# A Strassen block's accumulating transfer behind the next block's operand sums, and its transpose as a work list of its own

## The chip, the cores and the metric

The kernel runs on one core of a Trainium2 chip. The metric is the device time of one execution in microseconds (us), taken as the median of several runs; lower is better. A profile is one more execution, recorded by the hardware profiler.

## The reference

Two layers follow each other. The first is a causal depthwise convolution over the sequence: eight heads of 24 channels, seven taps per head, the taps normalized by a softmax. The second is a feed-forward layer with exact Gelu, 192 to 2048 to 192 channels.

```python
# x: (8, 4096, 192), weight: (8, 7), w_in: (192, 2048), w_out: (2048, 192), float32
w = exp(weight - max(weight)); w = w / (sum(w) + 1e-9)      # per head
out = einsum('hk,bskhg->bshg', w, windows of 7 of x padded in front)
h = out.reshape(32768, 192) @ w_in
return (0.5 * h * (1 + erf(h / sqrt(2)))) @ w_out
```

## The kernel before

The 32768 tokens are taken as two halves that are worked on side by side, and each half is cut into 35 blocks: six of 256 tokens (numbers 0 to 5) and 29 of 512 (6 to 34). For each block n the stages are these, and different engines work on different blocks at one time.

- SP loads x into `xin` (`load`, L571) and stores results from `osb` (`store`, L591).
- VectorE transposes x (`trans`, L748) and does the convolution as seven multiply-add steps of two parts each (`conv`, L776, written c in the order). ScalarE does the first tap of most blocks (L865). GpSimd copies the six columns of overlap between blocks (`halo`, L670).
- TensorE multiplies by w_in (`mm1`, L992) in 16 slices per block. ScalarE's Gelu (L897) takes each slice from PSUM `hp` to `gT`.
- In the slices of block n, TensorE also multiplies block n - 1 by w_out: for most blocks in the plain way (`mm2_t`, L1070), and for the thirteen blocks of the list `ST` (8, 10, ..., 32) with one level of Strassen's scheme (`mm2_s`, L1130). So the even blocks hold `mm2_t` of an odd block, and the odd blocks hold `mm2_s` of an even one.

A Strassen block m needs sums of its Gelu outputs as matmul operands, kept in the four tiles `sst`: S1, S3, Dn and S4, where Dn is made from S1 and S4 from Dn. S1 and S3 have four parts each, Dn and S4 two. Five of these sums are done by DMA from GpSimd's queue: a plain copy of the first term (`st_dma`, L495), then an accumulating transfer of the second (L498), ten transfers in all. VectorE does the rest (`st_add`, L488): S1 parts 2 and 3, S3 part 3, and all of Dn and S4. TensorE meets them in the odd block: S1 at its start, S3 next, then S4 (from slice 6).

After the products, block m's results are put together. ScalarE copies four pieces (`st_copy`, L526: `gsm`, `p5s`, `uu` and the negated half of `uu`). VectorE adds in four steps (`st_post`, called POST 0 to 3 here: L535, L539, L542, L546). GpSimd issues three moves (`st_move`): p5s (L505), gsm (L507), and the accumulating `tq += uu` (L510, 256 KB). Then three 512-column tiles are transposed into `osb` (`st_evac`, L561): j = 2 from PSUM, j = 1 from `tq` after that accumulating transfer, and j = 0 from `gsm`. The plain blocks have three such transposes (`evac_t`, L376), which also free PSUM banks for the Strassen products.

Two orders are fixed by hand. VectorE's is the string `ORDER`: each letter takes the next entry of a list (t transpose, c convolution step, p POST, e evacuation, and 1, 3, d, 4 for the sums of S1, S3, Dn, S4). GpSimd's is a list sorted by (block, place): the halo copy of a block, then that block's gsm and tq moves of the Strassen block before, then the ten operand transfers. Every wait on a semaphore holds all that is queued behind it on the same engine. S_EV counts evacuations; `EVC[n]` is its value before block n's.

Of the kernel before, what the change touches and what calls it, by code (L numbers as in the profile page):

```python
# [11 lines left out]
def bass_lightweight_conv__then__act_gelu_exact_kernel(  # L12
# [23 lines left out]
    NA = 5  # L36
# [3 lines left out]
    NP = D // 64  # L40
# [26 lines left out]
    NG = [w // 128 for w in WS]  # L67
# [3 lines left out]
    M0, M1 = 6, NB - 1  # L71
    ST = list(range(M0 + 2, M1, 2))
# [3 lines left out]
    for n in range(NB):  # L76
        new = M0 <= n < M1
        PHC.append(PHC[n] + (0 if n in ST else 2 if new else 3 * NG[n] if n == 0 else NG[n]))
        MMC.append(MMC[n] + (1 if new else 2 * NG[n] if n == M1 else NG[n]))
        EVC.append(EVC[n] + (0 if n < NA else NP if new else NG[n]))  # L80

# [32 lines left out]
    def sem(name):  # L116
        return es.enter_context(nc.semaphore(name))
# [4 lines left out]
    with es:  # L122
# [65 lines left out]
        S_DP = sem("S_DP")  # L188
        BY_DMA = [("S3", 0), ("S1", 0), ("S3", 1), ("S1", 1), ("S3", 2)]
        DMAS = [(3, "S3", 0, 0), (4, "S1", 0, 0), (5, "S3", 0, 1), (7, "S3", 1, 0), (8, "S1", 1, 0),  # L190
                (8.1, "S1", 0, 1), (10, "S1", 1, 1), (11, "S3", 2, 0), (11.1, "S3", 1, 1), (13, "S3", 2, 1)]
        S_CP = {k: sem("S_CP_%s_%d" % k) for k in BY_DMA}
        S_AD = {k: sem("S_AD_%s_%d" % k) for k in BY_DMA}
        S_PS = sem("S_PS")
        S_GU = sem("S_GU")
        S_TQ = sem("S_TQ")

        block = es.enter_context(nc.Block())

# [106 lines left out]
        def wait_ev(e, m, g):  # L306

            if m < NA:
                e.wait_ge(S_EVA, G0[m] + g + 1)
            else:  # L310
                e.wait_ge(S_EV, EVC[m] + g + 1)

        def wait_banks(t, m, g):

            k = G0[m] + g
            if m < M0:
                if k >= 2:
                    t.wait_ge(S_EVA, k - 1)
            elif g % 2:
                t.wait_ge(S_GELU, SL0[NB] - 1 + g // 2)  # L320
            elif M1 - 1 in ST:
                i = ST.index(M1 - 1)
                t.wait_ge(*((S_AC, 4 * i + 3) if g == 0 else (S_EV, EVC[M1] - 2)))
                t.wait_ge(S_DP, 4 * i + 3 + g // 2)
            else:
                t.wait_ge(S_EV, EVC[M1] - 2 + g)
# [92 lines left out]
        def osb_t(m, j):  # L419
            return ap(osb[m % 2], j, [[8 * C, 128], [C // 2, TB // 32], [NP, 32]])  # L420
# [91 lines left out]
        def st_copy(a, m, k):  # L512

            def xb(r, w=TB):
                return bank(BK[m]["X"], r, w)

            if k == 0 and m != ST[0]:
                a.wait_ge(S_EV, EVC[ST[ST.index(m) - 1] + 1])
            if k < 3:
                st_done(a, m, ("P1", "P5", "P6")[k])  # L520
            else:
                a.wait_ge(S_AC, 4 * ST.index(m) + 3)
            dst, src = (
                (gsm[LO, :], xb(LO)), (p5s[UP, :], xb(UP)), (uu[LO, :], xb(LO)), (uu[UP, :], uu[LO, :]),
            )[k]
            a.activation(out=dst, in_=src, func=AF.Copy, scale=-1.0 if k == 3 else 1.0).then_inc(S_AC)  # L526
# [22 lines left out]
        def st_evac(v, m, j):  # L549
            i = ST.index(m)  # L550
            if j == 2:
                st_done(v, m, "DE")
                v.wait_ge(S_OUT[m % 2], OUTS[m - 2])
                src = bank(BK[m]["D"])
            elif j == 1:
                v.wait_ge(S_TQ, 16 * (i + 1))
                src = tq[:, :]
            else:
                v.wait_ge(S_DP, 4 * i + 4)
                src = gsm[:, :]  # L560
            v.transpose(osb_t(m, j), src).then_inc(S_EV)  # L561

        def load(e, n, qs=(0, 2, 1, 3), sm=None):
            mb = WS[n] // 32
# [10 lines left out]
        def store(e, m):  # L575
            if m < M0:
                for g in range(NG[m]):
                    wait_ev(e, m, g)
                    e.dma_start(
                        ap(  # L580
                            outt,
                            (OFF[m] + 128 * g) * C,
                            [[C, 128], [HALF * C, 2], [1, C]],
                        ),
                        ap(osb[m % 2], g * C, [[8 * C, 128], [4 * C, 2], [1, C]]),
                    ).then_inc(S_OUT[m % 2], 16)
                return
            wait_ev(e, m, NP - 1)
            for q in range(4):

                e.dma_start(  # L591
                    ap(
                        outt,
                        ((q // 2) * HALF + OFF[m]) * C + (q % 2) * (C // 2),
                        [[C, 32], [32 * C, WS[m] // 32], [1, C // 2]],
                    ),
                    ap(
                        osb[m % 2],
                        32 * q * 8 * C,
                        [[8 * C, 32], [C // 2, WS[m] // 32], [1, C // 2]],  # L600
                    ),
                ).then_inc(S_OUT[m % 2], 16)
# [1 line left out]
        TAPS = ((5, 8, 11), (10, 12, 15))  # L604
        ORDER = (
            "tccccccccccccctccctccccccccccccwtccccccccccccwwwwwctcccccccccccctcccccccccccccccccccccccccettceccccc"
            "cccccccccetccccecccccccetcecc1ccde13de44ccccccpctpcpeccccccccpccececet1cccde13de44cccccpcccptpcecccc"
            "ccccpccececet1cccde13de44cccccpcccptpceccccccccpccececet1cccde13de44cccccpcccptpceccccccccpccececet1"
            "cccde13de44cccccpcccptpceccccccccpccececet1cccde13de44cccccpcccptpceccccccccpccececet1cccde13de44ccc"
            "ccpcccptpceccccccccpccececet1cccde13de44cccccpcccptpceccccccccpccececet1cccde13de44cccccpcccptpceccc"  # L610
            "cccccpccececet1cccde13de44cccccpcccptpceccccccccpccececet1cccde13de44cccccpcccptpceccccccccpccececet"
            "1cccde13de44cccccpcccptpceccccccccpccecececc1ccde13de44ccccccpcppepeeeeeeeee"
        )
        AT_COPY = {0: (1, 6), 1: (1, 8), 2: (1, 13), 3: (2, 1)}

# [1 line left out]
        def _(g):  # L617
# [73 lines left out]
            for m in ST:  # L691
                for at, name, q, h in DMAS:
                    work.append(((m, at), st_dma, g, m, name, q, h))
                work += [((m + 1, 8.5), st_move, g, m, 0), ((m + 2, 2), st_move, g, m, 1), ((m + 2, 3), st_move, g, m, 2)]
            for _, op, *rest in sorted(work, key=lambda q: q[0]):
                op(*rest)

# [1 line left out]
        def _(v):  # L699
# [98 lines left out]
            for j in range(3, len(pieces(1))):  # L798
# [6 lines left out]
                "p": [(st_post, v, m, k) for m in ST for k in range(4)],  # L805
                "e": [(evac, v, M0 - 1, g) for g in range(NG[M0 - 1])],
            }
            for c, name in zip("13d4", NS):
                lanes[c] = [(st_add, v, m, name, q) for m in ST for q in BY_V[name]]
            for m in range(M0, M1):  # L810
                lanes["e"] += [(st_evac, v, m, 2 - j) if m in ST else (evac_t, v, m, j) for j in range(NP)]
            lanes["e"] += [(evac_half, v, g, 0) for g in range(NG[M1])]
            for c in ORDER:
                op, *rest = lanes[c].pop(0)
# [96 lines left out]
        def _(t):  # L911
# [135 lines left out]
            def mm2_t(m, ps, i):  # L1047

                w = WS[m]
                if i == 0:  # L1050
                    if m - 1 in ST:
                        s = ST.index(m - 1)
                        if ps == 0:
                            t.wait_ge(S_AC, 4 * s + 3)
                            t.wait_ge(S_DP, 4 * s + 3)
                        elif ps == 1:
                            t.wait_ge(S_EV, EVC[m] - 2)
                    elif ps < 2:
                        t.wait_ge(S_EV, EVC[m] - (1 if m == M0 else 2) + ps)
                    if ps > 0:  # L1060
                        t.wait_ge(S_PH, PHC[m] + ps)
                if ps == 0 and i % 4 == 0:

                    t.wait_ge(S_GELU, SL0[m] + i + 4)
                for hf in range(2):
                    j = UPLO[ps][hf]
                    r = slice(64 * hf, 64 * hf + 64)
                    for h in range(2):
                        c0 = (2 * i + h) * w
                        ins = t.matmul(  # L1070
                            bank(BK[m][j], slice(64 * h, 64 * h + 64), w),
                            ap(
                                wout,
                                64 * hf * NF * C + CH[h][i] * C + j,
                                [[NF * C, 64], [NP, 64]],
                            ),
                            gT[m % 2][r, c0 : c0 + w],
                            start=(i == 0 and (ps == 0 or (ps, hf) == (1, 1))),
                            stop=(i == NF - 1 and (ps == 2 or (ps, hf) == (1, 0))),
                            tile_position=(64 * hf, 64 * h),  # L1080
                        )
                if i == NF - 1:
                    ins.then_inc(S_MM2 if ps == 2 else S_PH)
# [94 lines left out]
            m = NB - 1  # L1178
# [67 lines left out]
```

## Time and profile before

| what | value |
|---|---|
| median of 3 runs | 671.94 us (670.77 to 674.0) |
| profiled execution | 676.62 us |
| its span, first to last instruction | 674.9 us |
| granted TensorE clock | 1.00 |
| busy share: PE, DVE, ACT, POOL | 99%, 91%, 88%, 28% |
| even blocks of the Strassen stretch (first Gelu to first Gelu) | 20.53 us |
| odd blocks of it | 19.88 to 22.12 us |

Span and times inside it come from the profiled execution; 1.7 us of its time lie outside the span. A busy share is an average over all stages. An entry such as "DVE sst L488 <- DMA sst<-gT" reads: VectorE sat idle before its instruction of line 488, which writes `sst`, until a DMA that writes `sst` from `gT` had landed.

### The profile page before, as it was taken

Reading aid. Unit: us, or ns where it says so; the run is one execution under the profiler, and the core shown is the slowest. Engines: PE = TensorE matmul, PEld = TensorE weight load, DVE = VectorE, ACT = ScalarE, POOL = GpSimd, SP = SyncE. Lnnn points to the kernel's source line nnn. Section 1 sums busy time; section 2 is a strip of 40 time slices with the busy share of each in tenths; the row PEclk is TensorE's granted clock in tenths of the full one; section 3 lists DMA queues with packets and bytes.
Section 4 is the critical chain, followed back from the end, with each engine's and each line's share of the span. In section 5 each row is a group of like instructions: output and inputs, shape, how many; then the busy total and the mean of one; then the engine's idle time right before and its main releaser. Section 6 shows DMA issues by size and latency. Waiting matters only on the chain.

```text
span 674.9 us, 27462 instructions
## 1 busy us (share of the span) xinstructions
PE 666.3 (99%) x12504; PEld 498.6 (74%) x12504; DVE 612.9 (91%) x704; ACT 594.4 (88%) x681; POOL 191.4 (28%) x230
## 2 busy tenths in 40 slices
PE   9899999999999999999999999999999999999998
PEld 8899655565676776767777777876777777777787
DVE  5999998889998999999999999999999999999621
ACT  8799988898897988989899898988989899898883
POOL 7000702314142151421414325051240514324000
DMA  9436352686945769467695776958578785746433
GB/s 155 107 87 140 73 107 58 137 168 155 188 121 116 171 152 191 126 126 162 152 196 131 153 160 127 194 125 180 127 147 173 164 166 147 143 111 153 101 73 94
DMA packets 159075, 93.72 MB, mean 139 GB/s; under 512 B 129088, under 2 KB 152448, under 8 KB 158960
## 3 DMA queue, kind: packets, MB, share of 16 engines
q1 hardware_dynamic: 129136, 49.37, 33.7%
q0 software_dynamic: 28704, 42.02, 28.9%
q8 instruction: 98, 1.61, 1.0%
q10 hardware_dynamic: 1120, 0.59, 0.3%
q14 instruction: 17, 0.14, 0.1%
HBM read 28.31 MB, written 25.17 MB: 79 GB/s over the span
## 4 chain that ended last, share of the span: by engine, by line
PE 77%; DMA 10%; ACT 5%; DVE 3%; POOL 2%; issue 2%; DVEq 0%; POOLq 0%
PE hp L992 38%; PE ob L1070 17%; PE ob L1130 16%; DMA sst<-gT 9%; PE ob L1032 4%; ACT gT L897 4%; DVE sst L488 1%; DMA xin<-in_x_dram 1%; PE ob L1186 1%; PE hp L1186 1%; DMA win<-in_moe_w_in_dram 1%; POOL sst L498 1%; ACT acc L865 1%; DVE acc L776 1%; ACT uu L526 1%
## 5 line engine op out<-in xcount | busy, mean ns | idle before, releaser
L897 ACT ACTIVATE gT<-hp 128x1024 bf16<-128x1024 f32 x510 | 514.0, 1021 | 67.0 <-PE hp L992 61.3
L992 PE MATMUL hp<-xc,win 64*64 64x512 bf16 (+2 forms) x6036 | 447.2, 366 | 1.1 <-DVE xc L776 1.0
L992 PEld LDWEIGHTS hp<-xc,win 64*64 64x64 bf16 (+1 forms) x6036 | 238.6, 106 | 86.0 <-ACT gT L897 7.7
L776 DVE SCALAR_TENSOR_TENSOR acc<-xT,wcol,acc 128x1024 f32<-128x1024 f32 (+1 forms) x330 | 298.0, 963 | 4.0 <-ACT acc L865 3.1
L1070 PE MATMUL ob<-gT,wout 64*64 64x512 bf16 x2880 | 205.0, 376 | 0.0
L1130 PE MATMUL ob<-gT,wout 64*64 64x512 bf16 x1248 | 174.1, 377 | 0.0
L1070 PEld LDWEIGHTS ob<-gT,wout 64*64 64x64 bf16 x2880 | 118.2, 118 | 39.9
L1130 PE MATMUL ob<-sst,wst 64*64 64x512 bf16 x624 | 131.2, 377 | 2.3 <-DVE sst L488 1.3
L498 POOL DMA_DIRECT2D sst<-gT x65 | 85.6, 1317 | 97.6 <-DMA sst<-gT 94.3
L1130 PEld LDWEIGHTS ob<-gT,wout 64*64 64x64 bf16 x1248 | 86.1, 118 | 18.6
L748 DVE STREAM_TRANSPOSE xT<-xin 128x1536 f32<-128x1536 f32 (+2 forms) x39 | 74.5, 1921 | 4.0 <-DMA xin<-in_x_dram 3.9
L488 DVE TENSOR_TENSOR sst<-gT,sst 128x2048 bf16<-128x2048 bf16 x52 | 61.9, 1213 | 8.0 <-DMA sst<-gT 7.3
L495 POOL DMA_DIRECT2D sst<-gT x65 | 54.8, 858 | 30.1 <-ACT gT L897 28.5
L1130 PEld LDWEIGHTS ob<-sst,wst 64*64 64x64 bf16 x624 | 53.2, 107 | 13.2 <-DVE sst L488 3.7
L776 DVE SCALAR_TENSOR_TENSOR xc<-xT,wcol,acc 128x1024 bf16<-128x1024 f32 (+1 forms) x66 | 61.7, 958 | 0.1
L670 POOL COPY xT<-xT 128x18 f32<-128x18 f32 x30 | 29.1, 971 | 113.6 <-DVE xc L776 106.3
L865 ACT ACTIVATE acc<-xT,wcol 128x512 f32<-128x512 f32 (+1 forms) x87 | 61.0, 702 | 0.0
L1130 PE MATMUL ob<-gT,wst 64*64 64x512 bf16 x208 | 57.5, 377 | 1.1 <-DVE tq L535 1.0
L376 DVE STREAM_TRANSPOSE osb<-ob 128x512 f32<-128x512 f32 x45 | 40.4, 901 | 12.2 <-PE ob L1070 12.1
L1130 PE MATMUL ob<-sst,wout 64*64 64x256 bf16 x416 | 45.6, 269 | 0.0
L1032 PE MATMUL ob<-wout,gT 64*128 64x192 bf16 x768 | 41.3, 243 | 0.8 <-issue 0.8
L505 POOL DMA_DIRECT2D p5s<-p5s x13 | 7.4, 571 | 113.8 <-ACT p5s L526 113.8
(74 smaller groups left out, 320.1 us busy)
## 6 DMA issues: line engine op xcount, KB each, us to landing
sst<-gT POOLq DMA_DIRECT2D x130, 256.0 KB, 4.4
out_dram<-osb SPq DMA_DIRECT2D x124, 192.0 KB, 4.0
xin<-in_x_dram SPq DMA_DIRECT2D x116, 192.0 KB, 4.2
tq<-uu POOLq DMA_DIRECT2D x13, 256.0 KB, 4.0
xin<-in_x_dram SPq DMA_DIRECT2D x18, 96.0 KB, 2.5
gsm<-uu POOLq DMA_DIRECT2D x13, 128.0 KB, 2.2
p5s<-p5s POOLq DMA_DIRECT2D x13, 64.0 KB, 4.8
wout<-in_moe_w_out_dram POOLq DMA_DIRECT2D x4, 192.0 KB, 5.0
```

The source lines that it names most:

```text
L376: v.transpose(osb_t(m, j), bank(BK[m][j])).then_inc(S_EV)
L488: v.tensor_tensor(out, one, two, ALU.add).then_inc(S_SA[NS.index(name)])
L495: e.dma_start(out, one).then_inc(S_CP[name, q], 16)
L498: e.dma_start(out, two, accum_op=ALU.add).then_inc(S_AD[name, q], 16)
L748: v.transpose(out, src).then_inc(S_TR)
L776: ins = v.scalar_tensor_tensor(dst, src, wk, a, op0=ALU.mult, op1=ALU.add)
L865: a.activation(out=acc[n % 2][:, p * TB : p * TB + w], in_=ap(xT[n % 2], p * XW + HX, [[NP * XW, 128], [1, w]]), func=AF.Copy, scale=wcol[ ...
L897: a.activation(out=ap(gT[n % 2], i * c * 2 * w, dst), in_=ap(ob, 2 * TB, [[4 * TB, 128], *src[1:]]) if u < SL0[1] and u % 3 == 2 else ap(h ...
L992: ins = t.matmul(hbuf(u, slice(fo, fo + fw), o, w), ap(win, f1, [[NP * F, 64], [2, fw]]), xc[n % 2][r, p * TB : p * TB + w], start=(p == 0 ...
L1032: ins = t.matmul(bb[sub], gT[m % 2][r, c0 : c0 + 128], wout[r, CH[sub][i] * C : (CH[sub][i] + 1) * C], start=(ph == 0 and k == 0), stop=(p ...
L1070: ins = t.matmul(bank(BK[m][j], slice(64 * h, 64 * h + 64), w), ap(wout, 64 * hf * NF * C + CH[h][i] * C + j, [[NF * C, 64], [NP, 64]],), ...
L1130: ins = t.matmul(bank(BK[m][bk], slice(64 * cg, 64 * cg + 64), w), wt_, a[r, c0 : c0 + w], start=(e == mine[0]), stop=(e in (mine[-1], GRO ...
```

## The change

The accumulating transfer `tq += uu` of Strassen block m was issued by GpSimd ahead of the ten operand transfers of block m + 2. It now stands behind the last of them (place 14.1 in place of 3; the last operand transfer's place is renumbered from 13 to 14). Only the last Strassen block, which has no successor, keeps its place.

The transpose that reads `tq` leaves the list of evacuations, in which it stood between j = 2 and j = 0. It becomes a list of its own, q, with a semaphore of its own, S_ET. In `ORDER` it comes between the two S4 sums of block m + 2 (for block 30 behind both). In the same string one convolution step moves from behind the S4 sums to ahead of the first Dn sum, the next x transpose comes before the first bank's transpose in place of behind it, and the second bank's transpose comes behind S1 part 3.

S_EV now counts two evacuations for a Strassen block, and the waits on it are renumbered. The store of a Strassen block waits for S_ET as well, and so does ScalarE's first copy of the next Strassen block.

```diff
-        EVC.append(EVC[n] + (0 if n < NA else NP if new else NG[n]))
+        EVC.append(EVC[n] + (0 if n < NA else 2 if n in ST else NP if new else NG[n]))
...
-                (8.1, "S1", 0, 1), (10, "S1", 1, 1), (11, "S3", 2, 0), (11.1, "S3", 1, 1), (13, "S3", 2, 1)]
+                (8.1, "S1", 0, 1), (10, "S1", 1, 1), (11, "S3", 2, 0), (11.1, "S3", 1, 1), (14, "S3", 2, 1)]
...
             if k == 0 and m != ST[0]:
                 a.wait_ge(S_EV, EVC[ST[ST.index(m) - 1] + 1])
+                a.wait_ge(S_ET, ST.index(m))
...
-            v.transpose(osb_t(m, j), src).then_inc(S_EV)
+            v.transpose(osb_t(m, j), src).then_inc(S_ET if j == 1 else S_EV)
...
-            wait_ev(e, m, NP - 1)
+            wait_ev(e, m, (1 if m in ST else NP - 1))
+            if m in ST:
+                e.wait_ge(S_ET, ST.index(m) + 1)
...
     one period of ORDER:
-    pccececet1cccde13de44cccccpcccptpcecccccccc
+    pcccectec1cccd1e3de4q4ccccpcccptpcecccccccc
...
-                work += [((m + 1, 8.5), st_move, g, m, 0), ((m + 2, 2), st_move, g, m, 1), ((m + 2, 3), st_move, g, m, 2)]
+                work += [((m + 1, 8.5), st_move, g, m, 0), ((m + 2, 2), st_move, g, m, 1)]
+                work.append(((m + 2, 3 if m == ST[-1] else 14.1), st_move, g, m, 2))
...
+            lanes["q"] = [(st_evac, v, m, 1) for m in ST]
...
-                lanes["e"] += [(st_evac, v, m, 2 - j) if m in ST else (evac_t, v, m, j) for j in range(NP)]
+                lanes["e"] += [(st_evac, v, m, j) for j in (2, 0)] if m in ST else [(evac_t, v, m, j) for j in range(NP)]
...
-                            t.wait_ge(S_EV, EVC[m] - 2)
+                            t.wait_ge(S_EV, EVC[m] - 1)
```

More of the change, by code (lines that the diff above doesn't have):

```diff
@@ L196, in bass_lightweight_conv__then__act_gelu_exact_kernel @@
         S_TQ = sem("S_TQ")
+        S_ET = sem("S_ET")
         block = es.enter_context(nc.Block())
@@ L322, in wait_banks @@
                 i = ST.index(M1 - 1)
-                t.wait_ge(*((S_AC, 4 * i + 3) if g == 0 else (S_EV, EVC[M1] - 2)))
+                t.wait_ge(*((S_AC, 4 * i + 3) if g == 0 else (S_EV, EVC[M1] - 1)))
                 t.wait_ge(S_DP, 4 * i + 3 + g // 2)
@@ L606, in bass_lightweight_conv__then__act_gelu_exact_kernel @@
             "tccccccccccccctccctccccccccccccwtccccccccccccwwwwwctcccccccccccctcccccccccccccccccccccccccettceccccc"
[L607 to L612, printed above, removed]
+            "cccccccccetccccecccccccetcecc1ccde13de44ccccccpctpcpeccccccccpcccectec1cccd1e3de4q4ccccpcccptpcecccc"
+            "ccccpcccectec1cccd1e3de4q4ccccpcccptpceccccccccpcccectec1cccd1e3de4q4ccccpcccptpceccccccccpcccectec1"
+            "cccd1e3de4q4ccccpcccptpceccccccccpcccectec1cccd1e3de4q4ccccpcccptpceccccccccpcccectec1cccd1e3de4q4cc"
+            "ccpcccptpceccccccccpcccectec1cccd1e3de4q4ccccpcccptpceccccccccpcccectec1cccd1e3de4q4ccccpcccptpceccc"
+            "cccccpcccectec1cccd1e3de4q4ccccpcccptpceccccccccpcccectec1cccd1e3de4q4ccccpcccptpceccccccccpcccectec"
+            "1cccd1e3de4q4ccccpcccptpceccccccccpcccececc1ccde13de44qccccpcccppepeqeeeeeee"
         )
```

## The prediction

> **What bounds the kernel now.** First the page: busy times, then the chain that ended last.
>
> ```profile
> PE 666.3 (99%) x12504; PEld 498.6 (74%) x12504; DVE 612.9 (91%) x704; ACT 594.4 (88%) x681; POOL 191.4 (28%) x230
> PE 77%; DMA 10%; ACT 5%; DVE 3%; POOL 2%; issue 2%; DVEq 0%; POOLq 0%
> ```
>
> TensorE carries the chain, so only time in which TensorE waits can be won. It can hardly be read from 99%, so I cut the span at the first Gelu of each 512-token block. Even blocks take 20.53 us, all of them. Odd blocks, in which TensorE runs the Strassen products of the block before, take 20.06 us undisturbed; six take longer. One of each (a stretch, its length, busy time by engine):
>
> ```profile
> core 0: us, PE busy (x) PEld busy (x) DVE busy (x) ACT busy (x) POOL busy (x), PEclk, DMA share, GB/s
> 210.05:232.17 22.12, 20.86 (x393) 14.44 (x388) 20.13 (x22) 18.81 (x23) 2.47 (x4) 1.00 0.80 168
> 500.12:520.18 20.06, 20.06 (x393) 15.24 (x388) 19.87 (x22) 18.81 (x23) 2.42 (x4) 1.00 0.83 176
> ```
>
> Block 27 (from 500.12) is TensorE without a hole; block 13 (from 210.05) loses 2.06 us. The other losers are blocks 11, 15, 17, 23 and 25 with 1.19, 1.15, 1.58, 0.46 and 0.68: 7.1 us in all, over a floor of 674.9 - 7.1 = 667.8 us of span. That is the most that can be won. Below, times with a sign count from the first Gelu of the odd block.
>
> Who ends TensorE's waits between 150 and 310 us:
>
> ```profile
> DVE sst L488 <- DMA sst<-gT: 6.7, 4, 2.5
> PEld ob L1130 <- DVE sst L488: 3.2, 4, 0.8
> PEld ob L1130 <- DVE tq L535: 2.7, 4, 0.7
> PEld ob L1130 <- DMA sst<-gT: 2.6, 4, 1.2
> ```
>
> So VectorE's sums wait for the DMA sums, and TensorE for both. VectorE in block 13, then GpSimd:
>
> ```profile
> 206.31 2.63 DVE L776 SCALAR_TENSOR_TENSOR acc<-xT,wcol,acc 128x512 f32<-128x512 f32 x3
> 211.42 1.23 DVE L488 TENSOR_TENSOR sst<-gT,sst 128x2048 bf16<-128x2048 bf16 x1 [2.48 <-DMA sst<-gT]
> 212.56 0.89 DVE L376 STREAM_TRANSPOSE osb<-ob 128x512 f32<-128x512 f32 x1
> 213.33 1.24 DVE L488 TENSOR_TENSOR sst<-gT 128x1024 bf16<-128x1024 bf16 x2
> 216.40 2.29 DVE L488 TENSOR_TENSOR sst<-gT,sst 128x2048 bf16<-128x2048 bf16 x2
> 218.63 4.98 DVE L776 SCALAR_TENSOR_TENSOR acc<-xT,wcol,acc 128x1024 f32<-128x1024 f32 x5
> 223.64 0.69 DVE L535 TENSOR_TENSOR tq<-ob,p5s 64x512 f32<-64x512 f32 x1
> ```
> ```profile
> 192.03 0.95 POOL L510 DMA_DIRECT2D tq<-uu  x1
> 193.45 0.74 POOL L495 DMA_DIRECT2D sst<-gT  x1 [0.47 <-ACT gT L897]
> 205.49 1.20 POOL L498 DMA_DIRECT2D sst<-gT  x1 [3.35 <-DMA sst<-gT]
> 212.32 1.20 POOL L498 DMA_DIRECT2D sst<-gT  x1 [3.67 <-DMA sst<-gT]
> ```
>
> VectorE idles 2.48 us before the first Dn sum (211.42), until the accumulate of S1 part 1 (issued at 205.49) has landed. The sums after it and POST 0 (L535, 223.64) are late by as much. Over the odd blocks one rule fits: the loss is the end of POST 0 less 12.22. Ends of 13.42, 14.28, 13.38, 13.81, 12.69 and 12.91 give 1.20, 2.06, 1.16, 1.59, 0.47 and 0.69, against the six losses above; ends of 12.22 or less lose nothing. POST 0 is VectorE's end of a chain that is full but for two waits, on the S1 accumulate and, a period earlier, on the p5s move ahead of POST 1 (L539). Without idling, POST 0 ends 3.64 before the end of POST 1 of the last period (15.30 to 11.64, 16.33 to 12.69).
>
> **The change part by part.**
>
> *The tq transfer goes from ahead of the ten operand transfers to behind them.* GpSimd itself gains nothing: it issued the transfer in 0.95 us and then waited another 0.47 us for the Gelu. What goes is the transfer's share of the DMA engines at -18.0 to -13.3 (landing 3.3 to 4.7 us after issue, median 4.0, by the tile's view). The S3 copy issued 1.4 us behind it lands after 4.9, 4.5, 4.5 and 3.9 us in the losers 11 to 17; in blocks 29 and 31, where tq had landed early (3.3 us), after 2.65. Its accumulate, and the three transfers behind that, follow. In those two blocks the S1 accumulate lands at -3.38 and -3.06; in block 9, where no tq transfer stands ahead, at -2.49; in blocks 11 to 17 at +0.39, +1.25, +0.34 and +0.79. I take -2.5, the row without the transfer; the bounds are -3.4 and no change. The first Dn sum is due at about -0.2 (next point), so the idle before it goes: 1.63, 2.48, 1.20, 1.35, 0.79 us in blocks 11, 13, 15, 17, 25. What is left of those losses comes from the p5s move.
>
> *VectorE's order.* The tq transpose (0.90 us, 0.80 with the overlap) leaves its place before the last convolution step and comes between the two S4 sums; one convolution step (1.28, 1.21 with the overlap) moves from behind the sums to ahead of the first Dn sum; the second bank's transpose moves behind S1 part 3. No instruction is added or dropped between POST 3 and the next POST 0, so the end of POST 0 stays as it was, less the idle that goes. Inside, with POST 0 at 12.22: first Dn sum 1.21 - 0.80 = 0.4 later, at -0.2; S1 part 3 0.7 earlier behind Dn; S4 part 0 ends at 5.46 + 0.44 = 5.9 in place of 5.46; S4 part 1 at 7.8 in place of 6.6. TensorE wants S4 part 1 at 7.57 (the matmul's start in block 27), so at 7.50. VectorE must then be 0.3 us earlier than before: POST 0 due at 11.93 instead of 12.22, so p5s must land at 15.07 instead of 15.36. Its landings, less each block's loss, were 14.29 to 15.81. The excess over 15.36 adds up to 0.9 us, over 15.07 to 2.7. Cost: 1.8 us. The other bound is nothing, if the move lands a little sooner.
>
> *The new wait.* The transpose now waits for a transfer issued right behind the last S3 accumulate. Behind it on VectorE are S4 part 1 and all else; TensorE waits for that, and ScalarE's copy of P1 (slice 6, at 7.18) for the transpose. The transfer: S3's last accumulate was issued at -0.7 to +0.9 in the blocks without a wait, -1.46 in block 9; +0.72 for the next issue (spacing of back-to-back issues); 3.3 to 4.7 us to land. So 2.5 (from -1.46) to 6.3; with issue at +0.1 and 4.0, 4.8. It is due at 5.6 (7.50 less 1.1 and 0.8). Cost nothing at 4.8; at 6.3, 0.7 per block. A shorter chain ahead moves it down. One more sign of caution: in the losers a single one of the 16 engine rings posts 1 to 2 us after the other 15, close to the 16 KB packets of the instruction queue; such a packet falls at +4 to +5 in most odd blocks.
>
> The Trainium skill has a rule against such a place: "SBUF — State Buffer", section "SBUF: two separate sides", says that a DMA issued by GpSimd is starved of descriptors while VectorE holds the shared port pair in a two-port mode. Here the last S3 accumulate is issued amid the same VectorE sums and landed 3.62 to 3.67 us later in every block looked at, so the trace does not show it. By that rule the time would be that of the slower rival, 676.5.
>
> *Store and semaphore.* SP's store of the Strassen block waits for the transpose at about 6.7. It was issued at 6.3 behind a load's four issues, so it and the load and store behind it move by 0.5 us; the load's data is used more than 20 us later. Nothing. The later GpSimd halo copy (0.95 us at +2) feeds a convolution step at about +17. Nothing. S_ET's added waits on ScalarE and SP pass at once. The tail keeps its order and is TensorE's. Nothing.
>
> **Sum.** Profiled execution: 7.1 - 0.9 (what p5s causes) = 6.2 us of losses go and 1.8 come: -4.4 us, 676.62 to 672.2. The median of the runs, 671.94, lies 4.7 below that execution. If it lies there because those runs wait less, only a third of the losses is in it (2.4 of 7.1) and the gain is 1.5 (4.4 x 2.4 / 7.1); if the profiling costs the difference elsewhere, 4.4. I take 3.5, nearer to the view from which the sum is read: 668.4.
>
> **The rivals.**
> *The chain stays late* (no change). The straggling ring, not the tq transfer, may set it: the S1 accumulate itself took 4.9 to 5.8 us in the losers against 3.65, long after tq had landed. Against: block 9. Then the idle moves, and S4 part 1 costs what S1 part 3 wins: about 671.5. The same result comes if the earlier sums are eaten by the 0.3 us that S4 part 1 lacks.
> *The transfer lands late* (slower). One mechanism: VectorE's queue stops at the transpose in every Strassen period, from a landing at 5.6 on. At 6.3 it is 0.7 x 11 periods = 8 us: 676.5. For it: three transfers of one queue in flight ahead, SP's loads from 3.7 on, VectorE at 40.0 busy of 40.6 us per period, with no room for a new wait. Against: the arithmetic gives 4.8, and an earlier chain moves it further down.
>
> **How the numbers follow.** Chances: forecast 0.57, chain late 0.15, landing late 0.28. A half per cent, about what a measurement of this kernel can tell from no change, is 3.4 us. Of the forecast's own range (667 to 671) about two thirds is beyond that: faster 0.37, same 0.20 + 0.13 = 0.33, slower 0.28 + 0.02 = 0.30. The floor of span, 667.8, with its 1.7 outside, is 669.5 in the profiled execution; the runs may lie a few us below, so the low end is 666.8. The high end takes in the landing at 6.3: 677.
>
> **What would show it.** Right: blocks 11 to 17 near 20.1 to 20.5; the wait of L488 on sst gone; tq issued at about 0 and its transpose without idle before it; L535 waits by TensorE replaced by small ones on the S4 sum. Wrong: VectorE idle before L561 osb<-tq in most periods, with L1130 or ScalarE's L526 waiting behind it, or the first Dn sum still waiting at +0.5.

## The result, and the profile after

The changed kernel takes 676.95 us (median of 12 runs, 674.32 to 680.78). The kernel before, in the same runs, takes 672.83 (12 runs, 670.72 to 674.74). The ratio is 1.0064, 95% interval 1.0042 to 1.0086: slower by 0.6%, where 668.4 and a small gain were forecast. It lies just inside the upper end of the stated range (677), which had been put there for the slower rival.

The two profiled executions hide this: their spans are 675.2 us after and 674.9 before. The profiled execution after lies at the median of its runs. The one before, at 676.62, lies above all 12 of these runs of its kernel (later groups reach 677.1 at most, with medians of 672.5 to 674.2), so it was an execution with many waits. The waits are what has to be compared. Who waited in the changed kernel between 150 and 310 us (line numbers are a few higher than before: L489 the VectorE sums, L563 the transposes of a Strassen block, L528 ScalarE's copies, L1136 the Strassen products):

```profile
PEld ob L1136 <- DVE sst L489: 3.5, 3, 2.9
DVE osb L563 <- DMA tq<-uu: 2.8, 2, 2.2
PE ob L1136 <- DVE sst L489: 2.5, 1, 2.5
ACT gsm L528 <- DVE osb L563: 2.1, 1, 2.1
```

Two kinds of wait that led the list before are gone: VectorE's sums no longer wait for DMA sums (6.7 us before), and TensorE no longer waits for POST 0 (2.7 us before). In their place VectorE waits for the tq transfer, and TensorE and ScalarE wait behind it. The odd blocks 13, 27, 19 and 17 of the changed kernel (stretch, length, busy time by engine):

```profile
208.75:231.66 22.91, 20.45 (x394) 14.34 (x388) 19.69 (x23) 18.96 (x22) 3.68 (x5) 1.00 0.86 167
498.08:519.55 21.47, 20.46 (x394) 14.19 (x388) 18.36 (x21) 18.97 (x23) 4.17 (x5) 1.00 0.82 177
333.49:354.35 20.86, 20.46 (x394) 14.24 (x388) 19.64 (x22) 18.97 (x23) 2.91 (x3) 1.00 0.84 176
292.90:312.97 20.07, 20.07 (x394) 14.07 (x388) 18.28 (x21) 18.83 (x23) 1.83 (x5) 1.00 0.92 189
```

Block 17 is whole now; it lost 1.58 before. Blocks 27 and 19, which lost nothing before, lose 1.41 and 0.80, and block 13 loses 2.85 instead of 2.06. GpSimd ahead of block 13, and VectorE in it (a choice of the rows):

```profile
192.16 0.73 POOL L496 DMA_DIRECT2D sst<-gT  x1 [1.40 <-ACT gT L903]
203.16 1.19 POOL L499 DMA_DIRECT2D sst<-gT  x1 [2.58 <-DMA sst<-gT]
210.25 1.18 POOL L499 DMA_DIRECT2D sst<-gT  x1 [3.96 <-DMA sst<-gT]
210.96 1.39 POOL L511 DMA_DIRECT2D tq<-uu  x1
```
```profile
208.81 1.24 DVE L489 TENSOR_TENSOR sst<-gT,sst 128x2048 bf16<-128x2048 bf16 x1
213.74 1.20 DVE L489 TENSOR_TENSOR sst<-gT,sst 128x2048 bf16<-128x2048 bf16 x1
217.16 0.85 DVE L563 STREAM_TRANSPOSE osb<-tq 128x512 f32<-128x512 f32 x1 [2.22 <-DMA tq<-uu]
217.90 1.17 DVE L489 TENSOR_TENSOR sst<-gT,sst 128x2048 bf16<-128x2048 bf16 x1
219.00 3.79 DVE L781 SCALAR_TENSOR_TENSOR acc<-xT,wcol,acc 128x512 f32<-128x512 f32 x4
```

The first Dn sum (208.81) starts without idling. The tq transfer is issued at 210.96, right behind the last S3 accumulate, and lands 6.2 us later; the transpose waits 2.22 us for it, and S4 part 1 ends at 219.07, which is 10.32 us into the block. In block 19 there is no idle before the transpose, and S4 part 1 is late all the same:

```profile
338.71 1.20 DVE L489 TENSOR_TENSOR sst<-gT,sst 128x2048 bf16<-128x2048 bf16 x1
339.80 0.89 DVE L563 STREAM_TRANSPOSE osb<-tq 128x512 f32<-128x512 f32 x1
340.56 1.19 DVE L489 TENSOR_TENSOR sst<-gT,sst 128x2048 bf16<-128x2048 bf16 x1
```

It ends at 341.75, 8.26 into the block; TensorE wanted it 0.8 earlier. Two blocks before, VectorE had idled 1.66 us ahead of POST 1 for the p5s move, and the new place of S4 part 1 leaves less slack for that. Over the eleven odd blocks from 11 to 31 one rule fits: the loss is the end of S4 part 1 less 7.47. Ends of 7.85, 10.32, 7.61, 7.30, 8.26, 7.92, 7.85, 8.12, 8.88, 8.11 and 7.85 stand against losses of 0.38, 2.85, 0.15, 0.01, 0.80, 0.45, 0.38, 0.66, 1.41, 0.64 and 0.39 us. The sum is 8.1 us. VectorE idles 5.4 us before the transpose (0.55, 2.22, 0.86, 1.73 and 0.07 in blocks 11, 13, 25, 27, 31). In blocks 11, 25 and 27 the idle is longer than the loss. Taken off each block's loss as far as it goes, it explains 4.7 us. The other 3.4 follow the p5s move, by the due time of 15.07 that the prediction worked out for the new order: in blocks 11, 13, 17, 19, 21, 27 and 29 it landed, less the block's own loss, 0.64, 0.23, 0.86, 0.43, 0.37, 0.64 and 0.30 us after that, and the odd block behind each lost nearly as much without idle, 0.64, 0.15, 0.80, 0.45, 0.38, 0.64 and 0.32. Block 9 does not fit: an excess of 0.60, and block 11 would have lost nothing without its idle.

### The profile page after: what moved, and what is told of

Read it like the earlier page. It is cut to its first block, busy times and chain, and to the rows that moved or that the text cites. A ratio compares the mean times of both kernels' runs of the same rounds, so it can differ in the third digit from the quotient of the medians.

```text
span 675.2 us, 27463 instructions
## 1 busy us (share of the span) xinstructions
PE 666.1 (99%) x12504; PEld 462.8 (69%) x12504; DVE 611.7 (91%) x704; ACT 595.6 (88%) x681; POOL 196.0 (29%) x230
## 4 chain that ended last, share of the span: by engine, by line
PE 71%; DVE 9%; issue 8%; DMA 7%; POOL 4%; ACT 1%; SPq 0%; DVEq 0%; POOLq 0%; ACTq 0%
PE hp L998 36%; PE ob L1076 17%; PE ob L1136 13%; DVE acc L781 4%; PE ob L1038 4%; DVE sst L489 2%; DMA sst<-gT 2%; POOL sst L499 2%; DMA tq<-uu 2%; DMA xin<-in_x_dram 2%; DMA p5s<-p5s 1%; DVE xT L753 1%; PE ob L1192 1%; PE hp L1192 1%; DVE xc L781 1%
## 5 line engine op out<-in xcount | busy, mean ns | idle before, releaser
L998 PE MATMUL hp<-xc,win 64*64 64x512 bf16 (+2 forms) x6036 | 441.9, 366 | 1.1 <-DVE xc L781 1.0
L998 PEld LDWEIGHTS hp<-xc,win 64*64 64x64 bf16 (+1 forms) x6036 | 217.7, 106 | 105.5 <-ACT gT L903 8.2
L1076 PE MATMUL ob<-gT,wout 64*64 64x512 bf16 x2880 | 201.1, 376 | 0.0
L1136 PE MATMUL ob<-gT,wout 64*64 64x512 bf16 x1248 | 164.5, 376 | 0.0
L1076 PEld LDWEIGHTS ob<-gT,wout 64*64 64x64 bf16 x2880 | 106.8, 118 | 51.3
L1136 PE MATMUL ob<-sst,wst 64*64 64x512 bf16 x624 | 131.0, 376 | 0.0
L499 POOL DMA_DIRECT2D sst<-gT x65 | 82.2, 1265 | 71.5 <-DMA sst<-gT 70.8
L1136 PEld LDWEIGHTS ob<-gT,wout 64*64 64x64 bf16 x1248 | 79.8, 118 | 24.0
L674 POOL COPY xT<-xT 128x18 f32<-128x18 f32 x30 | 37.7, 1256 | 106.6 <-DVE xc L781 100.2
L496 POOL DMA_DIRECT2D sst<-gT x65 | 50.9, 783 | 52.2 <-ACT gT L903 51.9
L489 DVE TENSOR_TENSOR sst<-gT,sst 128x2048 bf16<-128x2048 bf16 x52 | 62.6, 1207 | 0.0
L1136 PE MATMUL ob<-gT,wst 64*64 64x512 bf16 x208 | 57.4, 376 | 0.0
L1136 PEld LDWEIGHTS ob<-sst,wst 64*64 64x64 bf16 x624 | 53.7, 107 | 5.0
L1136 PE MATMUL ob<-sst,wout 64*64 64x256 bf16 x416 | 46.4, 270 | 4.4 <-DVE sst L489 4.4
L1136 PEld LDWEIGHTS ob<-sst,wout 64*64 64x64 bf16 x416 | 34.8, 119 | 12.3 <-DVE sst L489 8.6
```

The costliest lines, as they stand in the source:

```text
L489: v.tensor_tensor(out, one, two, ALU.add).then_inc(S_SA[NS.index(name)])
L496: e.dma_start(out, one).then_inc(S_CP[name, q], 16)
L499: e.dma_start(out, two, accum_op=ALU.add).then_inc(S_AD[name, q], 16)
L674: g.tensor_copy(dst, src).then_inc(S_HALO)
L998: ins = t.matmul(hbuf(u, slice(fo, fo + fw), o, w), ap(win, f1, [[NP * F, 64], [2, fw]]), xc[n % 2][r, p * TB : p * TB + w], start=(p == 0 ...
L1076: ins = t.matmul(bank(BK[m][j], slice(64 * h, 64 * h + 64), w), ap(wout, 64 * hf * NF * C + CH[h][i] * C + j, [[NF * C, 64], [NP, 64]],), ...
```

## The experiments

Theory A was that S4 part 1 comes too late, because the tq transpose and its wait stand ahead of it. Its rivals were that the moved transfer disturbs other transfers (B), that the new waits on S_ET cost (C), and that only the late landing counts (D). "Loss" below is the sum over the odd blocks from 11 to 31 of what each takes over 20.06 us, in the one profiled execution, which is not always near the median of its runs. Ratios are against the kernel before, run on the same chip; medians of different rows can come from different chips, so the ratios are what has to be compared. The four groups of runs together give:

| kernel | median us | ratio to before (95%) | loss us |
|---|---|---|---|
| before (first profile) | 672.83 | 1 | 7.1 |
| changed | 676.95 | 1.0064 (1.0042 to 1.0086) | 8.1 |
| before again | 673.68 | 0.9986 (0.9963 to 1.0009) | 4.0 |
| transpose behind S4 | 670.38 | 0.9949 (0.9927 to 0.9971) | 1.0 |
| transfer at its old place | 674.96 | 1.0019 (1.0004 to 1.0033) | 7.4 |
| convolution step back | 683.17 | 1.0132 (1.0098 to 1.0167) | 11.8 |
| transpose before POST 0 | 668.36 | 0.9946 (0.9925 to 0.9968) | 0.0 |
| the same again | 669.20 | 0.9929 (0.9903 to 0.9955) | 0.5 |
| transpose before POST 0, old transfer place | 670.73 | 0.9957 (0.9940 to 0.9974) | 2.8 |
| transpose behind S4, old transfer place | 669.62 | 0.9966 (0.9950 to 0.9983) | 1.5 |
| transpose behind S4, ScalarE waits at copy 0 | 673.56 | 1.0024 (1.0008 to 1.0039) | 5.2 |
| 16 warm-up matmuls | 677.47 | 1.0055 (1.0029 to 1.0082) | 10.7 |
| ScalarE waits at copy 2, else as changed | 679.56 | 1.0076 (1.0040 to 1.0112) | 8.4 |

**A second look at the kernel before.** No edit.

> The kernel before, unchanged, for a second profile. If the first profile (span 674.9 us, 7.1 us of TensorE waits in the odd blocks) was an execution with more waits than usual, this one shows a span of 669 to 673 us and 1.5 to 5 us of such waits, with the first Dn sum waiting less for the S1 accumulate. If the first profile was typical and profiling itself costs 4 us, it shows 674 to 675 again, with 7 us of waits.

Its span is 671.5 us and its loss 4.0. So the first profile was an execution with more waits than usual; profiling did not add the difference. The same six blocks lose (1.00 and 1.51 in blocks 15 and 17), with block 31 and 0.14 beside them, but blocks 11 and 13 lose 0.31 and 0.10 instead of 1.20 and 2.06.

**The transpose behind both S4 sums.**

```diff
-        )
+        ).replace("4q4cccc", "44qcccc")          # ORDER
...
             if k == 0 and m != ST[0]:
                 a.wait_ge(S_EV, EVC[ST[ST.index(m) - 1] + 1])
+            if k == 2 and m != ST[0]:
                 a.wait_ge(S_ET, ST.index(m))
```

> The changed kernel with the tq transpose behind both S4 sums in place of between them, and ScalarE's wait for it at the copy that overwrites uu (slice 13) in place of the first copy (slice 6). Theory A (the loss is S4 part 1 coming after 7.47 us, because the transpose and its wait stand ahead of it): S4 part 1 ends at or under 7.5 in nearly all odd blocks, TensorE no longer waits for L489, and the time falls to 671 to 673 us, at or under the kernel before. Theory B (the moved transfer slows other transfers, p5s and loads, so that VectorE is late whatever the place of the transpose): 675 to 677 us, unchanged. Theory C (the new waits on S_ET and the store cost): a part, 674 to 675.

It falls below both kernels, and just below the range that was expected for theory A. S4 part 1 ends at 6.41 to 7.25 except for 7.61 in block 13. This is theory A, and rival B falls: the transfer stands where the change put it. Of the waits that this argument is about, little is left between 150 and 640 us:

```profile
PEld ob L1137 <- DVE tq L538: 1.2, 3, 0.6
DVE osb L564 <- DMA tq<-uu: 0.6, 1, 0.6
DVE sst L489 <- DMA sst<-gT: 0.3, 1, 0.3
PEld ob L1137 <- DVE sst L489: 0.2, 1, 0.2
```

**The transfer back at its old place, VectorE's order as changed.**

```diff
-                work.append(((m + 2, 3 if m == ST[-1] else 14.1), st_move, g, m, 2))
+                work.append(((m + 2, 3), st_move, g, m, 2))
```

> The changed kernel with the tq transfer back ahead of the operand transfers; VectorE's order stays changed. Theory A has two parts: late landings (idle before the transpose, 5 us in the profile) and the order alone (0.8 for the transpose and 1.2 for the convolution step ahead of S4 part 1, 3 us). So no idle before the tq transpose, but S4 part 1 still late by 0.3 to 0.8 in most blocks, more where the S1 accumulate lands late: 674 to 676 us. Rival D (the loss is only the late landing): 672 to 673, like the kernel before.

VectorE has no idle before the transpose, and the loss is still 7.4. The tile's view of tq has no line for its own transfer any more, and yet TensorE waits 6.9 + 2.9 us for L489:

```profile
PEld ob L1136 <- DVE sst L489: 6.9, 10, 1.1
PE ob L1136 <- DVE sst L489: 2.9, 7, 0.6
DVE sst L489 <- DMA sst<-gT: 2.3, 3, 1.3
```

The same rule holds: S4 part 1 ends at 7.03 to 8.76, the loss is that end less 7.47. Rival D falls; the place costs without a late landing of tq, here on top of S1 accumulates that land late again (VectorE idles 1.33 and 0.78 us for them in blocks 11 and 15).

**The convolution step back behind the sums.**

```diff
-        )
+        ).replace("ectec1cccd1e3de4q4cccc", "ectec1ccd1e3de4q4ccccc")
```

> The changed kernel with the one convolution step put back behind the S4 sums; the transpose stays between them and the transfer behind. Theory A: S4 part 1 ends 1.2 us earlier in the blocks in which the transpose does not idle, so these lose nothing, and the blocks in which the transfer lands after 5.6 lose as before: 673 to 675 us, some 3 under the changed kernel. Rival D (only the landing counts): no difference to the changed kernel, 676 to 677.

This missed: it got slower by 1.3%, the worst of all. S4 part 1 did come earlier in the blocks without idle (6.81 to 6.98). But the step had been filling time. Without it VectorE reaches the sums earlier and then stands, for the last Gelu before S1 part 3 and for the tq transfer, and has the step still to do before POST 0:

```profile
PEld ob L1136 <- DVE tq L537: 8.5, 11, 1.2
DVE osb L563 <- DMA tq<-uu: 7.4, 6, 2.5
DVE sst L489 <- ACT gT L903: 4.8, 9, 0.8
```

Now TensorE waits for POST 0 (L537), and the rule of the kernel before returns: the loss is the end of POST 0 less 12.22 (15.08 in block 31 for a loss of 2.86). So the moved step was not a cost only. From the landing, 0.8 + 1.1 us, five steps and POST 0 (together 7.6) had to fit before 12.22, which puts the due time of the landing at 4.6 instead of 5.6.

**The transpose shortly before POST 0.**

```diff
-        )
+        ).replace("4q4ccccp", "44ccqccp")
...
+                if i:
+                    v.wait_ge(S_ET, i)           # POST 0
```

with ScalarE's wait at copy 2 as above.

> As the version with the transpose behind both S4 sums, but with the transpose two convolution steps further back, shortly before POST 0, which overwrites tq (and POST 0 waits for S_ET in words). There the transfer may land up to about 9 us after the block's start, later than any landing seen (8.4). Theory A: VectorE never idles before the transpose, the 0.8 us that the version behind S4 still lost in its two blocks with late landings goes, and the time is 0 to 1 us under that version: 669.5 to 671. If late landings also hurt otherwise (through the store or ScalarE's copy of uu), nothing is gained: 671 or more.

> The version with the transpose shortly before POST 0 once more, beside the two others on one chip: 668 to 669 us and no loss in any odd block. Over 670 would mean that its first runs were lucky.

Both are faster than the kernel before, 668.36 and 669.20, by 0.54% and 0.71%, and neither is quite what was expected. The first is 1.1 us below its range. Its ratio, 0.9946, cannot be told from the 0.9949 of the version behind S4, so what the two further steps are worth is not shown by the runs' times. In its profile no odd block loses anything. The repetition is 0.2 us above its range, and two blocks lose: 0.20 in block 15 and 0.23 in block 27, by the rule of POST 0. In the first profile the transfer landed up to 8.8 us into a block (6.9 us after its issue), and nobody waited for it: the tile's view ends its list of waiters empty.

```profile
its engine sat idle before it (us, times) until:
  DMA p5s<-p5s: 3.3, 5
  PE ob L1139: 1.3, 1
who waited for it (us, times):
busy tenths in 40 slices 0000000000201002010010100102001010100110
DMA to landing us min/median/max: 3.3/4.4/6.9
```

**Which of the two won, the move or the order?** Both versions with the transpose behind, with the transfer at its old place.

> The version with the transpose behind both S4 sums, with the tq transfer back ahead of the operand transfers. It tells which of the two won: the transfer's move or VectorE's order. If the move (the prediction's first term): the S1 accumulate lands at -0.9 to +0.7 again in blocks 11 to 17, the first Dn sum idles, POST 0 ends after 12.22, and the time is 672.5 to 675, like the kernel before. If VectorE's order alone (S1 part 3 ahead of the second bank's transpose, the transpose out of the way of the sums): 670 to 671, like the version with the move.

> The version with the transpose shortly before POST 0, with the tq transfer back ahead of the operand transfers: the transfer's move alone, undone in the best version. If the move is worth what the prediction said under typical waits (1.5 us): 669.5 to 671, 1 to 2.5 over the best version, with the first Dn sum waiting in one or two blocks. If VectorE's order does it all: 668 to 668.8.

The larger part is the order. With the transfer at its old place they still take 0.34% and 0.43% less than the kernel before. The version with the old place has 0.9957, the repetition of the same order with the moved transfer, on the same chip, 0.9929: the move is worth 0.2 to 0.3% (1.5 us between the medians; the intervals of the two ratios overlap a little). In the first pair the difference (0.9949 and 0.9966, from two groups of runs) is within the intervals. The waits are what the prediction said they would be: the S1 accumulate lands at +0.60 and +0.72 in blocks 13 and 15, and the first Dn sum idles 1.05 and 1.50 us there:

```profile
DVE sst L489 <- DMA sst<-gT: 3.7, 5, 1.5
```

Those two blocks lose 0.95 and 1.03 of the 2.8 us. Block 27 loses the rest, because TensorE itself waits there for the last S3 accumulate, which landed 5.6 us after its issue. Which of the order's edits wins (S1 part 3 ahead of the second bank's transpose, the earlier convolution step, the later transpose) was not taken apart.

**ScalarE's wait.** Two kernels: the version with the transpose behind S4 with the wait left at ScalarE's first copy, and the changed kernel with only the wait moved to copy 2.

> The version with the transpose behind both S4 sums, with ScalarE's wait on S_ET back at its first copy (7.18 us into the odd block). There the transpose ended at 7.2 to 8.4, so ScalarE would stand 0 to 1.2 us (mean 0.45) in each odd block with the Gelus behind it. If ScalarE's slack takes it (18.8 us busy of 20.06): 670 to 671.5. If TensorE feels it: up to 0.45 x 11 = 5 us, 673 to 675.

> The changed kernel with ScalarE's wait on S_ET at the copy that overwrites uu instead of the first copy, and nothing else; the transpose stays between the S4 sums. If S4 part 1 alone sets the loss (theory A), ScalarE's wait at the first copy only stood where TensorE was late already: 675 to 678 us, like the changed kernel. If ScalarE's wait carries a part of its own: 672 to 675.

In the changed kernel the wait is not the cause: moving it alone gives 1.0076, no better than 1.0064 (the intervals overlap; the median of 679.56 lies above both ranges), and the S4 rule holds as before. Behind the S4 sums it is the next bound. There the loss is the start of copy 0 less 7.45 (8.72 and 8.67 in blocks 29 and 15 for 1.27 and 1.23), and the version gives up all it had won:

```profile
PEld hp L998 <- ACT gT L903: 15.5, 51, 0.8
ACT gsm L528 <- DVE osb L563: 6.6, 9, 1.4
PEld ob L1136 <- ACT gsm L528: 1.2, 4, 0.4
```

**Why the transfer lands late.**

```diff
-            for i in range(48):
+            for i in range(16):
                 t.matmul(hp[1][:, 0:128], one, one)
```

> The changed kernel with 16 instead of 48 warm-up matmuls at the start, which moves the 16 KB packets of TensorE's instruction queue by 64 of 256 instructions, some 1.7 us later against the blocks; no other stage is touched. If such a packet is what holds one of the 16 rings back: in blocks 23 to 31 the packets fall at about +6 in place of +4.3, and the last ring of the tq transfer, which now lags there by 0.3, 0.6, 2.0, 0.0 and 1.2 us, lags by less than 0.5 in most of them. If the lagging ring has another cause: the same lags in the same blocks. The time may go either way by 2 us, since other transfers meet the packets instead.

The semaphore records of the trace show the 16 posts of a DMA (one from each engine ring), the packet records show when the instruction queue moved its 16 KB packets. At its old place the fifteenth post of the tq transfer came 3.3 us after issue (3.6 in one block), half a us behind the 128 KB copy of gsm. At the new one, 0.7 us behind the S3 accumulate, it came after 4.2 in most blocks (4.0 to 5.5). That the accumulate ahead is what adds the 0.9 us was not tried. The last post came up to 2.0 us later still. In four of the five blocks in which VectorE idled for it (11, 25, 27, 31) the fifteenth post came before 5.6, so that only the last ring was late; in block 13 the transfer was issued late (+2.20) and all rings were.

With 16 warm-ups the packets of the instruction queue moved from +3.1 to +5.5 in blocks 23 to 31 to +4.8 to +6.7, and the lag of the last ring there went from 0.3, 0.6, 2.0, 0.0 and 1.2 to 0.6, 1.3, 0.2, 0.2 and 0.4. So three of the five lag by less than 0.5, as expected if the packet is the cause, and two do not. Block 25, where the lag grew, agrees as well: its transfer was issued at +2.6 and met the packet at +5.5. In blocks 11 to 15, where a packet now fell at +0.2 to +1.5, into the transfer's flight, the lag went from 0.4, 0.7 and 0.1 to 1.5, 1.3 and 1.3.

Over all 13 profiles the link is closer than this one experiment shows. Of the 169 tq transfers, 63 had a packet start 0.9 to 3.6 us after their issue, and in 62 of these the last post lags by more than 0.6 us. Where the packet started later in the flight, 6 of 52 do, and of the 15 transfers without a packet in flight none (0.41 at most). The bounds are read off the same transfers, so they are a description and no rule; a packet in the middle of the flight goes with a late ring nearly always, one near its end seldom.

The time itself stayed (1.0055). The profiled execution is the slowest of that kernel's ten runs (679.84), so its loss of 10.7 is not typical; in blocks 25 to 31 the tq transfer was issued at +1.7 to +2.6, where it had been -1.7 to +1.0, and landed late for that reason.

## Why the prediction was wrong

The direction was wrong. The mechanism that was to win time did occur, but it had less to win than the sum said, and the new wait, which the sum put at nothing, cost more.

- **What the move wins** was right as a mechanism. The S1 accumulate was put at -2.5; it landed at -1.96 to -3.64, mean -2.9, against a mean of -0.75 and -1.2 in the two profiles before. The idle before the first Dn sum is gone.
- **How much there was to win** was mis-sized. The term "6.2 of 7.1 us go" came from a profiled execution far above the median. With 1.7 us outside the span and the same floor, the median of 672.83 holds 3.3 us. The text saw the gap of 4.7 to the median and took it for the larger part as a cost of profiling; the second profile shows a loss of 4.0 at 673.24 us, so it was waits. The changed kernel has 3.4 us of loss that is not idle before the transpose. By these estimates there would have been next to nothing to win even without the new wait.
- **The new wait, "cost nothing at 4.8"**, is the step that failed. It priced one landing, and the mean landing was close to it, 4.92. That was partly luck: the transfer was issued 0.8 us sooner than the sum had it (+0.05 in the mean, against +0.1 + 0.72) and took 0.9 longer (4.87 against the 4.0 of its old place). What the sum left out was the spread. Landings went from 2.5 to 8.4, where the upper bound was 6.3. The due time of 5.6 was right: the five blocks whose transfer landed later than that are the five in which VectorE idled, 5.4 us, of which 4.7 are loss. The straggling ring, which made four of the five late, stood in the prediction as "one more sign of caution", without a price.
- **The order, 1.8 us**, had the right rule (S4 part 1 due at 7.50; measured 7.47) and a fair size: the sum left 0.9 + 1.8 = 2.7 us of loss, and 3.4 us were measured without the idle, because p5s landed later than in the profile before (an excess over 15.07 of 3.5 us from block 11 on, by the sum's own rule). The transpose between the sums made the due time tight in most blocks, and the prediction named this and then let the idle that goes outweigh it.
- **S_ET's wait on ScalarE, "passes at once"**, was wrong in blocks 13 and 27 (2.7 us), but TensorE was late there already; alone it moves nothing. Once the transpose stands behind the S4 sums, the same wait carries a loss of 5.2 us. **The store, "nothing"**, was right as far as the waits of the changed kernel show; it was not tried by itself.
- **The slower rival** had the mechanism and nearly the time (676.5), at 0.28. That the time fits so well is luck: the rival had VectorE stop in all 11 periods for 8 us, and it stopped in five for 5.4, with the order's cost beside it. It was held down by the sum for an average landing. The loss is one-sided, the excess over a due time, and so it is set by the late landings.
- The rule of the Trainium skill ("SBUF — State Buffer", section "SBUF: two separate sides") says that a DMA issued by GpSimd is starved of descriptors while VectorE holds the port pair that the two share in a two-port mode. The runs do not show that here: in nine of the eleven blocks the first post of the tq transfer came 3.97 to 4.03 us after issue, whether it was issued amid the Dn sums (block 17) or amid the convolution steps before them (block 29), and in four of the five late blocks it was the last ring alone that was late.

## What to carry to other kernels

When a step moves behind other work and gains a new wait, take its landing time from rows with the same transfers ahead of it, not from its old place, and price each landing that comes after the due time, not the mean landing: only these cost, and an early one pays nothing back. Put the consumer of a transfer as late as the next writer of its buffer allows, and move a buffer's wait to the instruction that really overwrites it; here these two edits turned 0.6% of loss into 0.5 to 0.7% of gain. And before a sum is made from a profile, compare that execution with the runs: one with many waits overstates what can be won.

## What the runs showed that was not expected

The 16 KB packets of TensorE's instruction queue, about one per 6.9 us, go with a late ring: when one starts 0.9 to 3.6 us after a tq transfer's issue, the last of the 16 posts comes 0.6 to 2.2 us after the other fifteen (62 of 63 transfers). The waiting instruction needs all 16 posts, so a late ring holds VectorE. In the two profiles of the kernel before, the packet in the first third of each odd block falls within about 1 us of the same place, so the same blocks are hit again; 64 instructions fewer at the start moved the packets to other places.

A version with less VectorE work ahead of a wait was slower: the convolution step that looked like a delay was filler for two waits.

The p5s move landed after 3.5 to 3.7 us (mean) in the three profiles with the transpose before POST 0, and after 4.3 to 4.9 in all others. There the store of the Strassen block, which waits for the transpose, is issued at 9.2 to 9.6 us into the block in the mean instead of 6.7 to 7.9, so its packets come behind the p5s move. That the one causes the other was not tried.
